# The last query chunk of a fused attention and FFN block, divided into two halves

## The chip, the cores and the metric

The kernel runs on one core of one Trainium2 chip. The metric is device time in microseconds (us) of one execution; a number of runs is taken and their median compared. Busy times, waits and clocks come from one profiled execution, a little apart from the runs.

## The reference

Input x has 2048 tokens of 512 numbers, in bf16. With layernorm without weights:

```python
x = A_x
h = x + _A_ref(_layernorm(x, axis=-1), A_wqkv, A_wo)      # 32 heads of 16, softmax over all 2048 keys
h2 = h + _B_ref(_layernorm(h, axis=-1), B_w_gate, B_w_up, B_w_down)

# _A_ref
scores = jnp.einsum("bhqd,bhkd->bhqk", q, k) * (Dh ** -0.5)
p = _softmax(scores, axis=-1)
o = jnp.einsum("bhqk,bhkd->bhqd", p, v)                   # then reshaped and multiplied by wo
# _B_ref, F = 1792
h = _sigmoid(g) * u                                       # g = x @ w_gate, u = x @ w_up
return jnp.einsum("bsf,fd->bsd", h, w_down)
```

## The kernel before

**Units and steps.** Queries are cut into four chunks of 512 (`QC`), the 32 heads into eight groups of four, the keys into 16 tiles of 128. A unit is one chunk, group, key tile and head: one score matmul (line 702) of 128 keys against 512 queries, which fills one PSUM bank. Units follow each other in the order chunk, group, key tile, head; three make a step, so there are 2048 units and 683 steps. A step's three banks lie in one of two score buffers `pss`, used in turn. ScalarE turns the three banks into bf16 probabilities with one exponential (line 711). In every fourth step, and in some more (the set `twice`), the third bank goes to VectorE instead, which works out the exponential in five operations spread over four steps (lines 730 to 743). The PV matmuls (line 769, four heads side by side in the array's columns, 17 columns each: 16 for values and one for the softmax sum) add into `acc`, mostly in one burst every fourth step.

**Queries in QB.** The score matmuls read their queries from one of two tiles `QB`, one for each head group in turn. It is filled by six DMAs on SyncE's queue: four for the rows (line 213) and two for a bound that is subtracted in the exponent (line 221). They are emitted while the group before is being scored, at its key tile 12 of 16.

**Normalising a group.** After the last PV matmul of a group, VectorE copies `acc` to `xs` (line 748). SyncE sends the four rows of sums to DRAM (`sd`), reads them back spread over the partitions (`s32`); five steps later VectorE takes reciprocals (line 757), and SyncE writes them to DRAM (`rd`) and spreads them by four DMAs (`rb`, line 762). Ten steps after the copy VectorE multiplies (line 763) into `OT`.

**Order of the work.** The program is written out by hand: a loop over steps emits a step's score matmuls, the PV matmuls due, what is due on VectorE and SyncE (`later`), then fillers. Each engine's queue, SyncE's among them, runs its instructions in that order. `emit_fill` takes fillers from one generator; `("at", n)` holds it until the next step with number n modulo 4, `("gap", n)` for n steps, `("from", n)` until step n.

**The FFN as filler.** Under the attention of a chunk, from its 16th step on, the output projection, layernorm, gate, up and down of the chunk before run as fillers (`ffn_tasks`). All their matmuls write to one PSUM bank, `pm`. wo: two halves of four matmuls and a transpose for each of four token tiles. Gate and up: 14 blocks of 128 rows of F; four gate matmuls in a step 3, a tanh on ScalarE (line 496), four up matmuls in the next step 1, a product on VectorE (line 500). Down: five matmuls in a cycle of four steps. Nothing is left to hide the last chunk's FFN: `ffn_last` runs it behind the loop, with six PSUM banks. Of the last chunk's first token tile seven of eight wo matmuls are done inside the loop (`wo_early`); `spin` issues matmuls whose results are not used.

Of the kernel before, what the change touches and what calls it, by code (L numbers as in the profile page):

```python
# [2 lines left out]

# [14 lines left out]
def kernel(  # L18
# [11 lines left out]
    nc = tc.nc  # L30
# [10 lines left out]
    TQ = QC // P  # L41
    NQC = S // QC
# [64 lines left out]
    stg = const.tile([P, 2 * S], BF16)  # L107
    stages = [stg[:, 0:S], stg[:, S:2 * S]]
# [97 lines left out]
    qgs = [(qc, g) for qc in range(NQC) for g in range(NG)]  # L206

    def emit_q_rows(n):
        qc, g = qgs[n]
        assert ("q", qc, g // 2) in ready  # L210
        for j in range(4):
            r = 64 * (g % 2) + DH * j
            nc.sync.dma_start(out=QB[n % 2][32 * j:32 * j + 32:2, j, :],
                              in_=QTu[r:r + DH, g // 2, qc * QC:(qc + 1) * QC])

    def emit_q_bound(n, engs=(nc.sync, nc.sync)):
        qc, g = qgs[n]
        assert ("b", qc, g // 2) in ready
        r = 32 * qc + 4 * g
        for h in range(2):  # L220
            engs[h].dma_start(out=QB[n % 2][64 * h + 1:64 * h + 2, 2 * h:2 * h + 2, :],
                              in_=bnd[r + 2 * h:r + 2 * h + 2, :])
# [151 lines left out]
    units = [(qc, g, kt, j) for qc in range(NQC) for g in range(NG) for kt in range(NT) for j in range(4)]  # L374
    groups = [units[i:i + GU] for i in range(0, len(units), GU)]
    NS = len(groups)
    SPC = NS / NQC

# [86 lines left out]
    def wo_mm(ps, t, g):  # L465
        nc.tensor.matmul(ps[:], lhsT=OT[t // TQ % 2][:, g, t % TQ * P:(t % TQ + 1) * P], rhs=wo_pad[:, g, :],  # L466
                         start=(g == 0), stop=(g == NG - 1))
# [18 lines left out]
    def gate_mm(ps, f, c):  # L486
        nc.tensor.matmul(ps[:], lhsT=wg[:, c, f * P:(f + 1) * P], rhs=hnT[:, c, :],  # L487
                         start=(c == 0), stop=(c == DC - 1))

    def up_mm(ps, f, c):  # L490
        nc.tensor.matmul(ps[:], lhsT=wu[:, c, f * P:(f + 1) * P], rhs=hnT[:, c, :],  # L491
                         start=(c == 0), stop=(c == DC - 1))
# [6 lines left out]
    def up_mul(ps, sg, f):  # L499
        nc.vector.scalar_tensor_tensor(out=hT[:, f, :], in0=sg[:], scalar=1.0, in1=ps[:],  # L500
                                       op0=ALU.add, op1=ALU.mult)
# [11 lines left out]
    def ffn_tasks(qc):  # L513
        yield ("rate", 8.0)
        for tt in range(TQ):
            xr = x_load(qc * TQ + tt)
            yield ("at", 3)
            ps = pm_tile()
            for g in range(NG):
                if g == NG // 2:  # L520
                    yield ("at", 1)
                yield 1
                wo_mm(ps, qc * TQ + tt, g)
# [5 lines left out]
        for f in range(FC):  # L529
            yield ("at", 3)  # L530
            psg = pm_tile()
            for c in range(DC):
                yield 1
                gate_mm(psg, f, c)
            sg = gate_act(psg)
            yield ("at", 1)
            psu = pm_tile()
            for c in range(DC):
                yield 1
                up_mm(psu, f, c)  # L540
            up_mul(psu, sg, f)
        for tt in range(TQ):
            for f in range(FC):
                if f % 5 in (0, 3):
# [5 lines left out]
            down_out(psd, qc * TQ + tt, tt)  # L550
        yield ("rate", None)
        yield ("gap", 1)
# [3 lines left out]
    def wo_early(qc):  # L556
        early[0] = pm_tile()
        for g in range(NG - 1):
# [3 lines left out]
            wo_mm(early[0], qc * TQ, g)  # L562
# [5 lines left out]
    def ffn_last(qc):  # L568
        t0 = qc * TQ
        sums, rb = pm_tile(), pm_tile()  # L570
        pss = [early[0]] + [pm_tile() for _ in range(TQ - 1)]
        tp = {}
        def wo(tt, g0, g1):
            for g in range(g0, g1):
                wo_mm(pss[tt], t0 + tt, g)
# [4 lines left out]
        wo(1, 0, NG - 1)  # L580
        xs = norm.tile([P, QC], FP32, name="xs")
        nc.vector.tensor_copy(out=xs[:], in_=acc[:])
        for q in range(TQ):
            nc.tensor.matmul(sums[:, 4 * q:4 * q + 4], lhsT=xs[:, q * P:(q + 1) * P],
                             rhs=ident_f[:, DH:P:32], start=True, stop=True)
        r16 = small.tile([P, 4 * TQ], FP32, name="r16")
        nc.vector.reciprocal(out=r16[:], in_=sums[:, 0:4 * TQ])
        rx = norm.tile([P, TQ, 4, 32], FP32, name="rb")
        wide = r16[:].rearrange("p (t j) -> p t j", j=4).unsqueeze(3).to_broadcast([P, TQ, 4, 32])
        nc.vector.tensor_copy(out=rx[:, 0:2], in_=wide[:, 0:2])  # L590
        nc.scalar.copy(out=rx[:, 2:4], in_=wide[:, 2:4])
        xrs = [x_load(t0 + q) for q in range(TQ)]
        wo(2, 0, NG - 1)
        for tt in range(TQ):
            nc.tensor.matmul(rb[:, tt * P:(tt + 1) * P], lhsT=rx[:, tt].rearrange("p j d -> p (j d)"),
                             rhs=ident_f[:], start=True, stop=True)
        nc.vector.tensor_tensor(out=OT[qc % 2][:, NG - 1, :], in0=xs[:], in1=rb[:], op=ALU.mult)
        add_x(0)
        add_x(1)
        wo(3, 0, 2)  # L600
        wo(0, NG - 1, NG)
        wo(1, NG - 1, NG)
        wo(3, 2, NG - 1)
        add_x(2)
        add_x(3)
        wo(2, NG - 1, NG)
        wo(3, NG - 1, NG)
        spin(acc, 5)
        mv = small.tile([P, TQ, nc.vector.BN_AGGR_DIM], FP32, name="mvl")
        nmr = small.tile([P, TQ], FP32, name="nmr")  # L610
# [13 lines left out]

        def turn(tt, copy):
            if tt % 2 == 0:
                tp[tt // 2] = pm_tile()[:].bitcast(BF16).rearrange("p (h b q) -> p h b q", h=2, b=4)
            pt = tp[tt // 2][:, tt % 2]
# [7 lines left out]
        stats(2)  # L636
# [3 lines left out]
        stats(3)  # L640
        apply(2)
        turn(1, nc.scalar.copy)
        spin(acc, 3)
        apply(3)
        turn(2, nc.vector.tensor_copy)
        spin(acc, 3)
        turn(3, nc.vector.tensor_copy)
        spin(acc, 2)
        for tt in range(TQ):
            nc.vector.tensor_copy(out=h_sb[:, tt, :], in_=pss[tt][:])  # L650
        for f in range(FC):
            psg = pm_tile()
            for c in range(DC):
                gate_mm(psg, f, c)
            sg = gate_act(psg)
            psu = pm_tile()
            for c in range(DC):
                up_mm(psu, f, c)
            up_mul(psu, sg, f)
        psd = [pm_tile() for _ in range(TQ)]  # L660
        for tt in range(TQ):
            for f in range(FC):
                down_mm(psd[tt], f, tt)
            down_out(psd[tt], t0 + tt, tt)

    def filler():
# [21 lines left out]
    def emit_scores(i):  # L688
# [8 lines left out]
        for ui, (qc, g, kt, j) in order:  # L697
            n_qg = qc * NG + g
# [3 lines left out]
            nc.tensor.matmul(pss[:, ui, :], lhsT=KT[rows, g, kt * P:(kt + 1) * P],  # L702
                             rhs=QB[n_qg % 2][rows, j, :], start=True, stop=True,
                             tile_position=(h0, 0) if pairs else None)
# [3 lines left out]
        k = i % 7  # L708
        pt = pt4[k] if k < 4 else (pt_early if i < GM else pt_late)[k - 4]
# [36 lines left out]
    def emit_norm(qc, g, i):  # L746
        xs = norm.tile([P, QC], FP32, name="xs")
        nc.vector.tensor_copy(out=xs[:], in_=acc[:])  # L748
        sd = dram.tile([4, QC], FP32, name="sd")
        for j in range(4):  # L750
            nc.sync.dma_start(out=sd[j:j + 1, :], in_=xs[32 * j + DH:32 * j + DH + 1, :])
        s32 = norm.tile([P, 16], FP32, name="s32")
        nc.sync.dma_start(out=s32[:], in_=sd[:].rearrange("j (a b) -> (j a) b", b=16))

        def recip():
            r32 = norm.tile([P, 16], FP32, name="r32")
            nc.vector.reciprocal(out=r32[:], in_=s32[:])
            rd = dram.tile([4, QC], FP32, name="rd")
            nc.sync.dma_start(out=rd[:].rearrange("j (a b) -> (j a) b", b=16), in_=r32[:])
            rb = norm.tile([P, QC], FP32, name="rb")  # L760
            for j in range(4):
                nc.sync.dma_start(out=rb[32 * j:32 * j + 32, :], in_=rd[j:j + 1, :].to_broadcast([32, QC]))
            later(i + 10, lambda: nc.vector.tensor_tensor(out=OT[qc % 2][:, g, :], in0=xs[:], in1=rb[:], op=ALU.mult))
        later(i + 5, recip)

    def emit_pv(qc, g, kt, i):
        assert ("v", kt) in ready
        for j in range(4):
            nc.tensor.matmul(acc[32 * j:32 * j + VW, :], lhsT=Vaug[:, kt, 4 * g + j, :],  # L769
                             rhs=p_of.pop((qc, g, kt, j)), start=(kt == 0), stop=(kt == NT - 1),  # L770
                             tile_position=(0, 32 * j))
        if kt == NT - 1 and (qc, g) != qgs[-1]:
            emit_norm(qc, g, i)


# [73 lines left out]
    with tc.manual_schedule():  # L849
# [32 lines left out]
        ffn_last(NQC - 1)  # L882
# [30 lines left out]
```

## Time and profile before

| What | Value |
|---|---|
| Median of 3 runs | 972.46 us (972.37 to 974.98) |
| Span of the profiled execution | 970.6 us; the profile lists no other time of its own |
| ScalarE busy | 894.9 us (92%) |
| TensorE busy | 836.9 us (86%), 5288 matmuls |
| VectorE busy | 798.0 us (82%) |
| GpSimd busy | 39.7 us (4%) |
| Mean granted TensorE clock | 0.998 |
| Score matmuls, line 702 | 2048 of 128x512, mean 381 ns |
| Exponentials on ScalarE, line 711 | 683 of 128x1536 or 128x1024 |
| tanh, line 496 | 56, mean 628 ns |
| QB rows, line 213 | 128 DMAs of 16 KB |

A matmul's duration holds its way through the array: matmuls that follow each other start closer together than they last. PE is TensorE's matmuls, PEld its weight loads, DVE VectorE, ACT ScalarE, POOL GpSimd, SP SyncE. Idle time of an engine that is not the bottleneck costs nothing. SPq marks the issue of a DMA on SyncE's queue; the transfer goes on after it.

### The profile page before, as it was taken

The numbers are of one execution on the slowest core, as the hardware profiler recorded it, in microseconds if no ns is written. First come the engines' busy times: TensorE is split into PE (matmuls) and PEld (weight loads), VectorE is DVE, ScalarE is ACT, GpSimd is POOL, SyncE is SP. The second block draws the span as 40 slices with busy tenths as digits, with TensorE's granted clock in tenths as the row PEclk, the third lists the DMA queues.
The fourth block names the chain that finished last, engine by engine and source line by source line (L and its number), as shares of the span: only waits on it lengthen the run. The fifth ranks groups of instructions, "written<-read, shape, count | busy, mean of one in ns | idle before, by whom it ended". The sixth has DMA issues, their size and how long they took to land.

```text
span 970.6 us, 14758 instructions
## 1 busy us (share of the span) xinstructions
PE 836.9 (86%) x5288; PEld 273.4 (28%) x5288; DVE 798.0 (82%) x1418; ACT 894.9 (92%) x773; POOL 39.7 (4%) x45
## 2 busy tenths in 40 slices
PE   4788888888888999988788999888788999998898
PEld 2221222222222232222222333222222223222343
DVE  9389999888878888889888888889878888889452
ACT  4799999999999999999999999999999999999731
POOL 4600000000000000000000000000000000000000
PEclk9999999999999999999999999999999999999999
DMA  5001341000003000000000000000000000000100
GB/s 160 20 1 56 113 94 37 15 16 5 16 23 101 15 15 16 20 19 28 4 26 27 16 16 15 21 8 26 16 26 26 16 16 14 8 25 24 34 2 22
DMA packets 32354, 28.07 MB, mean 29 GB/s; under 512 B 14300, under 2 KB 26716, under 8 KB 32280
## 3 DMA queue, kind: packets, MB, share of 16 engines
q1 hardware_dynamic: 30692, 25.56, 9.4%
q10 hardware_dynamic: 1588, 1.58, 0.5%
q8 instruction: 41, 0.67, 0.3%
q14 instruction: 33, 0.27, 0.1%
HBM read 20.18 MB, written 2.61 MB: 23 GB/s over the span
## 4 chain that ended last, share of the span: by engine, by line
PE 42%; DVE 28%; ACT 22%; issue 5%; DMA 2%; SPq 0%; ACTq 0%; POOL 0%; DVEq 0%
PE pss L702 20%; ACT pt L711 12%; PE acc L769 8%; ACT wd L711 4%; PE pm L491 4%; ACT stg L711 4%; DVE stg L730 4%; PE pm L487 3%; PE pm L504 2%; ACT QTu L711 2%; DVE pt L743 2%; DVE y L739 2%; DVE reg L733 2%; PE pm L466 2%; DVE st L130 2%
## 5 line engine op out<-in xcount | busy, mean ns | idle before, releaser
L702 PE MATMUL pss<-QB,KT 64*128 64x512 bf16 (+1 forms) x2048 | 470.8, 381 | 94.3 <-ACT pt L711 44.2
L711 ACT ACTIVATE pt<-pss 128x1536 bf16<-128x1536 f32 (+1 forms) x392 | 498.3, 1359 | 13.0 <-PE pss L702 10.7
L702 PEld LDWEIGHTS <-KT 64*128 64x128 bf16 (+1 forms) x2048 | 138.4, 95 | 377.6 <-issue 258.6
L711 ACT ACTIVATE stg<-pss 128x1536 bf16<-128x1536 f32 (+1 forms) x140 | 182.1, 1354 | 2.4 <-PE pss L702 0.9
L730 DVE TENSOR_SCALAR stg<-pss 128x512 int32<-128x512 f32 x123 | 84.7, 688 | 69.3 <-PE pss L702 58.5
L769 PE MATMUL acc<-pt,Vaug 128*17 128x512 bf16 x1175 | 113.0, 382 | 8.3 <-DVE xs L748 5.6
L711 ACT ACTIVATE wd<-pss 128x1536 bf16<-128x1536 f32 (+1 forms) x80 | 103.8, 1394 | 1.4 <-PE pss L702 1.3
L711 ACT ACTIVATE QTu<-pss 128x1024 bf16<-128x1024 f32 (+1 forms) x71 | 95.3, 1343 | 0.5 <-PE pss L702 0.2
L736 DVE SCALAR_TENSOR_TENSOR y<-reg 128x512 f32<-128x512 f32 x123 | 85.2, 693 | 4.2
L739 DVE SCALAR_TENSOR_TENSOR y<-y,reg 128x512 f32<-128x512 f32 x123 | 84.1, 684 | 1.1
L769 PEld LDWEIGHTS <-Vaug 128*17 128x17 bf16 x2048 | 39.3, 88 | 114.5 <-issue 96.6
L487 PE MATMUL pm<-reg,reg 128*128 128x512 bf16 x224 | 57.8, 380 | 6.0 <-DVE reg L500 6.0
L504 PE MATMUL pm<-wd,reg 128*128 128x512 bf16 x224 | 60.8, 381 | 0.5 <-DVE reg L500 0.5
L491 PE MATMUL pm<-reg,wu 128*128 128x512 bf16 x224 | 57.9, 381 | 0.0
L733 DVE TENSOR_SCALAR reg<-stg 128x512 int32<-128x512 int32 x123 | 52.1, 423 | 2.5
L137 POOL TENSOR_TENSOR rs<-ve,pw_neg 128x1 f32<-128x1 f32 (+1 forms) x24 | 17.1, 713 | 880.8 <-DVE ve L135 879.0
L496 ACT ACTIVATE sg<-pm 128x512 f32<-128x512 f32 x56 | 35.2, 628 | 18.0 <-PE pm L487 18.0
L769 PE MATMUL acc<-stg,Vaug 128*17 128x512 bf16 x420 | 50.5, 385 | 0.5 <-DVE xs L748 0.2
L500 DVE SCALAR_TENSOR_TENSOR reg<-sg,pm 128x512 bf16<-128x512 f32 x56 | 38.2, 682 | 14.0 <-PE pm L491 13.3
L743 DVE SCALAR_TENSOR_TENSOR pt<-y,stg 128x512 bf16<-128x512 f32 x70 | 47.8, 682 | 1.9
L730 DVE TENSOR_SCALAR wd<-pss 128x512 int32<-128x512 f32 x45 | 30.9, 686 | 13.1 <-PE pss L702 12.8
L156 PE MATMUL pm<-reg 128*128 128x512 bf16 x124 | 37.6, 391 | 1.2 <-DVE km L164 0.7
(115 smaller groups left out, 711.0 us busy)
## 6 DMA issues: line engine op xcount, KB each, us to landing
rb<-rd SPq DMA_DIRECT2D x124, 64.0 KB
reg<-in_A_x_dram SPq DMA_DIRECT2D x8, 256.0 KB
QB<-QTu SPq DMA_DIRECT2D x128, 16.0 KB
xr<-in_A_x_dram SPq DMA_DIRECT2D x16, 128.0 KB
out_dram<-ob SPq DMA_DIRECT2D x16, 128.0 KB
sd<-xs SPq DMA_DIRECT2D x124, 2.0 KB
KT<-stg SPq DMA_DIRECT2D x7, 256.0 KB
reg<-in_B_w_gate_dram SPq DMA_DIRECT2D x4, 448.0 KB
```

What stands on the lines that cost most here:

```text
L487: nc.tensor.matmul(ps[:], lhsT=wg[:, c, f * P:(f + 1) * P], rhs=hnT[:, c, :], start=(c == 0), stop=(c == DC - 1))
L491: nc.tensor.matmul(ps[:], lhsT=wu[:, c, f * P:(f + 1) * P], rhs=hnT[:, c, :], start=(c == 0), stop=(c == DC - 1))
L500: nc.vector.scalar_tensor_tensor(out=hT[:, f, :], in0=sg[:], scalar=1.0, in1=ps[:], op0=ALU.add, op1=ALU.mult)
L504: nc.tensor.matmul(ps[:], lhsT=hT[:, f, tt * P:(tt + 1) * P], rhs=wd[:, f, :], start=(f == 0), stop=(f == FC - 1))
L702: nc.tensor.matmul(pss[:, ui, :], lhsT=KT[rows, g, kt * P:(kt + 1) * P], rhs=QB[n_qg % 2][rows, j, :], start=True, stop=True, tile_positio ...
L711: ex = nc.scalar.activation(out=pt[:, 0:na, :], in_=pss[:, 0:na, :], func=ACT.Exp, scale=DH ** -0.5 / QS)
L730: return nc.vector.tensor_scalar(out=e_bits, in0=src, scalar1=ONE_BITS, scalar2=0.0, op0=ALU.add, op1=ALU.max)
L733: nc.vector.tensor_scalar(out=e_man, in0=e_bits, scalar1=0x7FFFFF, scalar2=-0x40800000, op0=ALU.bitwise_and, op1=ALU.bitwise_or)
L736: nc.vector.scalar_tensor_tensor(out=e_pol, in0=m, scalar=PA, in1=m, op0=ALU.add, op1=ALU.mult)
L739: nc.vector.scalar_tensor_tensor(out=e_pol, in0=e_pol, scalar=PB, in1=e_man.bitcast(FP32), op0=ALU.add, op1=ALU.mult)
L743: nc.vector.scalar_tensor_tensor(out=dst, in0=e_pol, scalar=PC, in1=e_bits.bitcast(FP32), op0=ALU.add, op1=ALU.mult)
L769: nc.tensor.matmul(acc[32 * j:32 * j + VW, :], lhsT=Vaug[:, kt, 4 * g + j, :], rhs=p_of.pop((qc, g, kt, j)), start=(kt == 0), stop=(kt == ...
```

## The change

The last chunk of 512 queries is divided into two of 256, so there are five chunks. In these two, a score bank holds two key tiles of 256 queries: a unit takes two score matmuls of 256 columns, an exponential sees as many columns as before, and the PV matmuls are twice as many with half the columns. A head group there has 8 x 4 units in place of 16 x 4, 10.7 steps in place of 21.3, and each group has its own QB rows, bounds and normalisation as before, so there are 16 groups in the last 171 steps instead of 8. QB rows are asked for at three quarters of a group's units (k 6 of 8). The tiles for normalisation are allocated once; in the half chunks the groups use their halves in turn.

The FFN of chunk 2 (512 queries) runs under the first half, from its 12th step on, that of the first half under the second. wo, layernorm and down use denser slots there (`ffn_wo_tight`, and three slots of three down matmuls in a cycle of four steps); for the first half gate and up take three slots in a cycle, each of eight 256-column matmuls, which fill a bank with two blocks of F. `ffn_last` now has 256 queries. The extra exponentials on VectorE (`twice`) end 14 steps into the second half: four fewer.

In the built program steps 0 to 511 stand as before. The fillers end at step 679, but for four of the seven early wo matmuls, which stand behind the loop. In the half chunks SyncE's queue holds, for each group, the four `sd`, the `s32`, then either `rd` and four `rb` and after them the six QB transfers, or the six first.

```diff
+    CHUNKS = [(0, QC), (QC, QC), (2 * QC, QC), (3 * QC, QC // 2), (3 * QC + QC // 2, QC // 2)]
+    NC = len(CHUNKS)
...
     def emit_q_rows(n):
-        qc, g = qgs[n]
-        assert ("q", qc, g // 2) in ready
+        c, g = qgs[n]
+        q0, w = CHUNKS[c]
+        assert ("q", q0 // QC, g // 2) in ready
         for j in range(4):
             r = 64 * (g % 2) + DH * j
-            nc.sync.dma_start(out=QB[n % 2][32 * j:32 * j + 32:2, j, :],
-                              in_=QTu[r:r + DH, g // 2, qc * QC:(qc + 1) * QC])
+            nc.sync.dma_start(out=QB[n % 2][32 * j:32 * j + 32:2, j, 0:w],
+                              in_=QTu[r:r + DH, g // 2, q0:q0 + w])
...
+    def n_k(c):
+        return NT // per_bank(c)
+
+    units = [(c, g, k, j) for c in range(NC) for g in range(NG) for k in range(n_k(c)) for j in range(4)]
...
+    def ffn_up(c):
+        w = CHUNKS[c][1]
+        at = cycle((3, 1) if c + 2 < NC else (3, 0, 1))
+        for fs in blocks_of(w):
+            yield ("at", next(at))
+            psg = pm_tile()
+            for i, f in enumerate(fs):
+                for k in range(DC):
+                    yield w / QC
+                    ffn_mm(wg, psg, w, f, i, k)
             sg = gate_act(psg)
...
+                if tight:
+                    if f % 3 == 0:
+                        yield ("at", (3, 0, 1)[at % 3])
+                        at += 1
+                elif f % 5 in (0, 3):
                     yield ("at", 0 if f % 5 else 3)
...
-        for qc in range(NQC - 1):
-            yield ("from", int((qc + 1) * SPC) + 15)
-            yield from ffn_tasks(qc)
-        yield from wo_early(NQC - 1)
+        for c in range(NC - 1):
+            yield ("from", int(first_step(c + 1)) + (11 if c + 3 >= NC else 15))
+            yield from ffn_tasks(c)
+        yield from wo_early(NC - 1)
...
-        for ui, (qc, g, kt, j) in order:
-            n_qg = qc * NG + g
+        n_of = max(per_bank(u[0]) for u in group)
+        parts = [(ui, u, h) for h in range(n_of) for ui, u in order[:2] if h < per_bank(u[0])]
+        parts += [(ui, u, h) for ui, u in order[2:] for h in range(per_bank(u[0]))]
+        for ui, (c, g, k, j), h in parts:
+            n_qg = c * NG + g
+            w = CHUNKS[c][1]
+            kt = k * per_bank(c) + h
...
-            nc.tensor.matmul(pss[:, ui, :], lhsT=KT[rows, g, kt * P:(kt + 1) * P],
-                             rhs=QB[n_qg % 2][rows, j, :], start=True, stop=True,
+            nc.tensor.matmul(pss[:, ui, h * w:(h + 1) * w], lhsT=KT[rows, g, kt * P:(kt + 1) * P],
+                             rhs=QB[n_qg % 2][rows, j, 0:w], start=True, stop=True,
                              tile_position=(h0, 0) if pairs else None)
-            if kt == 12 and j == 3 and n_qg + 1 < len(qgs):
+        for c, g, k, j in group:
+            n_qg = c * NG + g
+            if k == n_k(c) * 3 // 4 and j == 3 and n_qg + 1 < len(qgs):
                 emit_q_rows(n_qg + 1)
                 emit_q_bound(n_qg + 1)
...
+    def emit_pv(c, g, k, i):
+        w = CHUNKS[c][1]
+        for h in range(per_bank(c)):
+            kt = k * per_bank(c) + h
+            assert ("v", kt) in ready
+            for j in range(4):
+                p = p_of[(c, g, k, j)]
+                nc.tensor.matmul(acc[32 * j:32 * j + VW, 0:w], lhsT=Vaug[:, kt, 4 * g + j, :],
+                                 rhs=p[:, h * w:(h + 1) * w], start=(kt == 0), stop=(kt == NT - 1),
+                                 tile_position=(0, 32 * j))
...
-        for n in range(n0, min(int((qc + 1) * SPC) + 16, G1 - 8)):
+        for n in range(n0, min(int((qc + 1) * SPC) + 16, int(first_step(NC - 1)) + 14)):
             if n % ((4 if n < n0 + 56 else 3) * CYC) == 0:
                 twice.add(n + 2)
```

In `emit_norm` the DMAs and VectorE operations are the same in number, on 256 columns in the half chunks. In `ffn_last` the loops over token tiles run over two tiles instead of four, and of the seven wo matmuls of the second tile three stand ahead of the sums and four behind.

More of the change, by code (lines that the diff above doesn't have):

```diff
@@ L2 @@
 from contextlib import ExitStack
+from itertools import cycle
 import concourse.bass as bass
@@ L484, in hn_transpose, with blocks_of, ffn_mm @@
         transpose4(hnT[:, :, tt * P:(tt + 1) * P], hn, copy)
[L486 to L491, printed above, removed]
+    def blocks_of(w):
+        return [tuple(range(f, f + QC // w)) for f in range(0, FC, QC // w)]
+    def ffn_mm(wt, ps, w, f, i, c):
+        nc.tensor.matmul(ps[:, i * w:(i + 1) * w], lhsT=wt[:, c, f * P:(f + 1) * P], rhs=hnT[:, c, 0:w],
                          start=(c == 0), stop=(c == DC - 1))
@@ L577, in add_x @@
         def add_x(tt):
             nc.tensor.matmul(pss[tt][:], lhsT=ident_bf[:], rhs=xrs[tt][:], start=False, stop=False)
[L580 to L583, printed above, removed]
+        wo(1, 0, 3)
+        xs = norm_part(xs_all, w, NG - 1)
+        nc.vector.tensor_copy(out=xs, in_=acc[:, 0:w])
+        for q in range(n):
             nc.tensor.matmul(sums[:, 4 * q:4 * q + 4], lhsT=xs[:, q * P:(q + 1) * P],
@@ L585, in ffn_last @@
                              rhs=ident_f[:, DH:P:32], start=True, stop=True)
[L586 to L592, printed above, removed]
@@ L593, in ffn_last @@
-        wo(2, 0, NG - 1)
-        for tt in range(TQ):
+        wo(1, 3, NG - 1)
+        r16 = small.tile([P, 4 * n], FP32, name="r16")
+        nc.vector.reciprocal(out=r16[:], in_=sums[:, 0:4 * n])
+        rx = norm_part(rb_all, w, NG - 1).rearrange("p (t j d) -> p t j d", t=n, j=4)
+        wide = r16[:].rearrange("p (t j) -> p t j", j=4).unsqueeze(3).to_broadcast([P, n, 4, 32])
+        nc.vector.tensor_copy(out=rx[:, 0], in_=wide[:, 0])
+        nc.scalar.copy(out=rx[:, 1], in_=wide[:, 1])
@@ L606, in ffn_last @@
[L606 to L610, printed above, removed]
+        nc.vector.tensor_tensor(out=OT[c % 2][:, NG - 1, 0:w], in0=xs, in1=rb[:, 0:w], op=ALU.mult)
+        ready.add(("o", c, NG - 1))
+        for tt in range(n):
+            add_x(tt)
+        for tt in range(n):
+            wo(tt, NG - 1, NG)
+        spin(acc, 6)
+        mv = small.tile([P, n, nc.vector.BN_AGGR_DIM], FP32, name="mvl")
@@ L761, in recip @@
             for j in range(4):
-                nc.sync.dma_start(out=rb[32 * j:32 * j + 32, :], in_=rd[j:j + 1, :].to_broadcast([32, QC]))
-            later(i + 10, lambda: nc.vector.tensor_tensor(out=OT[qc % 2][:, g, :], in0=xs[:], in1=rb[:], op=ALU.mult))
+                nc.sync.dma_start(out=rb[32 * j:32 * j + 32, :], in_=rd[j:j + 1, :].to_broadcast([32, w]))
+            later(i + 10, scale)
         later(i + 5, recip)
[L766 to L773, printed above, removed]
+    def emit_pv(c, g, k, i):
+        w = CHUNKS[c][1]
+        for h in range(per_bank(c)):
[6 more added lines that the diff above has]
+                                 tile_position=(0, 32 * j))
+        if k == n_k(c) - 1 and (c, g) != qgs[-1]:
+            emit_norm(c, g, i)
```

192 lines of the change are left out of this document (112 added, 80 removed).

## The prediction

> **What bounds the kernel now.** Four views, in this order: the page, the table by stage, the chain that ended last, and the SyncE queue's timeline.
>
> ```profile
> PE   4788888888888999988788999888788999998898
> ACT  4799999999999999999999999999999999999731
> ```
>
> ScalarE is full from the second slice to the last three, so the attention loop ends when its exponentials end. The last slices belong to TensorE. The table by stage (columns: us, busy PE, PEld, DVE, ACT, POOL, then granted clock, DMA share, GB/s) cuts the end where the chain of waits changes engine:
>
> ```profile
> 756.85:832.95 76.10, 71.40 (x450) 22.77 (x448) 63.49 (x109) 75.38 (x70) 0.00 (x0) 1.00 0.05 15
> 832.95:892.05 59.10, 53.92 (x348) 16.55 (x345) 52.05 (x88) 58.47 (x49) 0.00 (x0) 1.00 0.07 20
> 916.84:930.75 13.91, 13.32 (x79) 7.00 (x79) 7.26 (x23) 4.27 (x7) 2.16 (x4) 1.00 0.13 40
> 930.75:955.09 24.34, 24.34 (x113) 11.06 (x113) 11.18 (x17) 8.36 (x14) 0.00 (x0) 1.00 0.00 1
> 955.09:970.60 15.51, 12.09 (x56) 5.29 (x54) 3.45 (x5) 0.00 (x0) 0.00 (x0) 0.97 0.10 34
> ```
>
> The chain of waits names the borders:
>
> ```profile
> 915.70 1.14 ACT pt L711
> 955.09 12.10 PE pm L504 x56
> ```
>
> The last exponential ends at 916.84, and 53.8 us of tail follow to 970.6, in which TensorE works alone on the last 512 queries. Ahead of that, the first two rows show ScalarE 99% busy and TensorE 94% with gate and up fillers, 91% with down fillers: the loop has little room on either engine.
>
> **The tail gets shorter.** Gate and up: 28 groups in 24.34 us, 0.87 each; 256 queries need 14 groups of eight 256-column matmuls, as many columns as a group now, so 12.2 us: minus 12.2. Down: 56 matmuls in 12.1, 0.216 each; 28 remain: minus 6.0. The first 13.9 us: the per-head sums, reciprocals and OT scaling run on half the columns, and two of four LayerNorm tiles, each with about 1.1 us of DVE steps in a row, go; but the seven wo matmuls that now stand ahead of the sums partly remain. I take 9.5, minus 4.4. The final 3.4 (last sum and its store) stays. Total minus 22.6 (ends minus 21.5 and minus 23.5).
>
> That needs 256-column matmuls at half the price. Here is the row nearest to it:
>
> ```profile
> 26.40 0.61 PE L288 MATMUL pm<-reg 128*128 128x256 bf16 x4
> ```
>
> One of them alone lasts 0.27, so four in 0.61 start 0.11 apart, with a full weight load each. The Trainium skill, "TensorE: Matmul & The Clock Gate", Part 3, says that a weight load overlaps running matmuls only when the row group differs; by that each would show its 0.097 us load and the 14 groups would take about 11 us more. The trace disagrees: loads of the same rows are hidden here.
>
> **The loop gets heavier.** Both kernels have 683 steps, steps 0 to 511 stand alike, and every step exponentiates as many columns. What is added under the loop: seven tanh, the FFN matmuls of 256 queries (about 22 us of TensorE), less four extra DVE exponentials in the last half chunk. I price four-step cycles by rows, from the starts of the exponentials. Without fillers a cycle takes 5.05 to 5.09; with down fillers 4.97; with gate and up (eight matmuls) 5.37 to 5.50, one tanh being 0.4 of that. A cycle with an extra DVE exponential takes 4.55 to 5.1, but the cycle behind it often 5.7 to 6.1, so I count their removal as nothing.
> - Steps 648 to 664: three slots in a cycle where the gate and up cycles have two. TensorE: 5.1 now, plus four matmul times of 0.216, is 5.9; psum tile pm is single, so each up group also waits for the tanh one step ahead: 6.2. Four cycles, 24.8 against 19.8 now: plus 5.0.
> - Denser down (steps 604 to 628, 668 to 680): 9 matmuls in a cycle, about 5.3: plus 1.3. Denser wo and LayerNorm, at 5.3: plus 1.0.
> Together plus 7 (ends plus 2, if ScalarE alone set the pace, and plus 13, if every hand-over of pm stalls). The fillers do end inside the loop, at step 679.
>
> **The query rows come late.** This is the largest term. A head group was 64 units, 21.3 steps; it is now 32, 10.7 steps, and has the same DMAs on SyncE: normalisation (four sd, s, rd, four rb), then four QB rows and two bounds. The rows of the next group are still asked for at three quarters of the group: four to five steps before their first use until now, one or two from now on. SyncE's queue goes in program order. One group of it in the timeline:
>
> ```profile
> 814.13 1.10 SPq L751 DMA_DIRECT2D sd<-xs  x4
> 816.22 0.34 SPq L753 DMA_DIRECT2D s<-sd  x1
> 819.75 0.34 SPq L759 DMA_DIRECT2D rd<-r  x1
> 821.17 1.71 SPq L762 DMA_DIRECT2D rb<-rd  x4
> 822.93 2.46 SPq L213 DMA_DIRECT2D QB<-QTu  x4
> 825.76 1.28 SPq L221 DMA_DIRECT2D QB<-bnd  x2
> ```
> ```profile
> 819.48 0.25 DVE L757 RECIPROCAL r<-s 128x16 f32<-128x16 f32 x1
> ```
>
> The first bound is issued 6.28 us after the reciprocal. What issue to use costs is seen where TensorE waits for one, at the start (SyncE issue, then the matmul):
>
> ```profile
> 32.25 0.70 SPq L221 DMA_DIRECT2D QB<-bnd  x1
> 34.13 0.37 PE L702 MATMUL pss<-QB,KT 64*128 64x512 bf16 x1 [0.72 <-DMA QB<-bnd]
> ```
>
> That is 1.88, so QB is usable 8.16 after the reciprocal. The reciprocal is emitted five steps after the norm, and this one started 0.6 ahead of its step's exponential. In the changed kernel's order, three cases take turns. In five of the groups (norm at steps 514, 546, 578, 610, 642) rd and rb stand ahead of the rows, and the new group begins three steps after the reciprocal, which is 4.04 us in this stretch. The exponential of that step is then late by 8.16 + 0.4 (its matmuls) - 0.6 - 4.04 = 3.9 us; other reciprocals lie up to 1.1 us on either side. TensorE stands at that score matmul, with the PV matmuls, all fillers and so VectorE's later work queued behind; ScalarE has nothing to read. Five times 4: plus 20. In five more (norm at 538, 570, 602, 634, 666) the rows stand ahead of rd, start when the s load is out, 3.1 us after the xs copy, and are usable about 8 us after the norm, six steps (7.6 to 8.1) being there: 0.5 each, plus 2.5. The others have a step more and wait for nothing. An out store (615) and an x load (636) that stand ahead of the rows add 0.5 each. Together plus 23.5. Nothing hides it; the ends are plus 14 (half-size transfers land sooner, and VectorE, rested, does its reciprocals a microsecond early) and plus 28. Below nothing is excluded, as the rows are never asked for earlier.
>
> **Clock.** Behind 36 us without fillers the granted clock fell, with no gap on TensorE over 1.1 us near it:
>
> ```profile
> 706.00:710.00 4.00, 2.69 (x21) 0.87 (x22) 3.64 (x7) 4.00 (x4) 0.00 (x0) 1.00 0.27 80
> 710.00:714.00 4.00, 3.73 (x19) 0.76 (x19) 2.62 (x5) 3.01 (x3) 0.00 (x0) 0.57 0.10 34
> ```
>
> The cycle around it took 6.19 where its neighbours take 5.08: 1.1 us for one drop. Five waits leave TensorE idle for over 4 us each; a wait may bring a drop or none, so 0 to 5.5, and I take two: plus 2. The Trainium skill, same page, "HAM oscillation", says that gaps beyond about 3.4 us halve the clock; by that all five would, plus 5.5. The drop here came without such a gap.
>
> **Sum.** -22.6 + 7 + 23.5 + 2 = +9.9. The span is 970.6, the profile gives no time around it, and the median of the runs, 972.46, lies 1.9 above it; I keep that. 970.6 + 9.9 + 1.9 = 982.4.
>
> **Rivals.**
> - *The rows come in time (faster).* If SyncE lets them out before rd, or TensorE is so far behind ScalarE that it asks later, the waits and drops go: 972.5 - 22.6 + 7 = 957. For it: no wait on QB shows after the start, and SyncE is idle for most of a group. Against: two score buffers keep TensorE at most two steps ahead, and SyncE's waits for the reciprocal stand in the rows above. It decides where the five waits and the 2.5 fall below 13 us together.
> - *Half the waits*, if groups with a wait push the next norm and reciprocal ahead of their step: 972.5 - 22.6 + 7 + 12 + 1 = 970, no change.
> - *TensorE pays more (slower still).* A quad of 256-column PV matmuls is not in the trace; a 512-column quad takes 0.216 (twelve matmuls, 0.65). If its four loads of 0.088 us set the pace, a half quad costs as much, 0.65 more in a cycle; in some 9 dense cycles, where TensorE sets the pace, plus 6; with five drops (plus 3.5 beyond my two), 992. For it: a half quad has half the time to hide its loads. Against: these loads start 3 ns apart, and L288 hides a 0.097 us load behind 256 columns.
>
> **How the numbers follow.** Forecast 0.70, rows in time 0.12, half the waits 0.10, TensorE 0.08. The forecast's own range, with its ends taken as independent (1, 5.5, 7 and 3 us, root of the squares 9.4), is 973 to 992. Down to 967 it takes in the half waits; rows in time are left out with the edges, some 0.2. A measurement of this kernel can tell about 0.3%, 2.9 us: slower is over 975.4, faster under 969.5. Of the forecast 0.64 is slower, 0.05 same, 0.01 faster; half the waits give 0.06 same and 0.04 faster. Slower 0.72, same 0.11, faster 0.17.
>
> **What would show it.** The chain of waits from the last exponential to the end 31 us, not 54: the tail. Score matmuls (the 256-column ones) with idle time "<-DMA QB<-bnd" or "QB<-QTu", five near 4 us and a few under 1, in all about 23: the rows; under 8 would make me wrong. ScalarE's idle time behind the score matmul of the same steps. Cycles in steps 648 to 664 near 6.2. The clock under 1 in some of the 4 us behind a wait. If the waits are there and the time is still lower, the loop's other terms were overpriced.

## The result, and the profile after

| | before | after |
|---|---|---|
| Median of the runs | 973.04 us (972.37 to 974.98, 4 runs) | 997.91 us (997.01 to 999.86, 4 runs) |
| Span of the profiled execution | 970.6 us | 995.7 us |
| Mean granted TensorE clock there | 0.998 | 0.982 |

The change makes the kernel slower: the ratio of the times is 1.026, with a 95% interval of 1.0241 to 1.0278. The direction and the places were foreseen, the size was not: plus 24.9 us where plus 9.9 was predicted, and above the range.

The rows of busy tenths of the page after, to be laid beside the two shown of before:

```profile
PE   4788888888888999987788999887788979798988
ACT  4799999999999999999999999999787979697872
PEclk9999999999999999999999999999898989899999
```

ScalarE, full to the last three slices before, now has five dents from slice 29 on. The clock row dips at the first four of them. The views of waits name what lies there. First, for what the score matmuls' engine sat idle, over the whole execution (us, times):

```profile
its engine sat idle before it (us, times) until:
  ACT pt L776: 39.5, 101
  DMA QB<-bnd: 21.9, 10
```

One of these ten is the wait at the start that both kernels have. The waits of all engines between 695 and 964 us (us in total, times, longest):

```profile
PE pss L765 <- DMA QB<-bnd: 21.1, 9, 4.4
...
ACT pt L776 <- PE pss L765: 18.9, 21, 4.7
...
ACT stg L776 <- PE pss L765: 13.8, 14, 4.5
```

TensorE waits 21.1 us for bounds of QB, and ScalarE waits for TensorE in the same steps. Of the nine waits five are long: 4.18, 4.25, 4.38, 4.37 and 2.23. One of them, as SyncE's queue and then TensorE's show it:

```profile
752.40 0.34 SPq L833 DMA_DIRECT2D rd<-r_all  x1
754.82 1.71 SPq L835 DMA_DIRECT2D rb_all<-rd  x4
756.58 2.46 SPq L221 DMA_DIRECT2D QB<-QTu  x4
759.08 1.26 SPq L231 DMA_DIRECT2D QB<-bnd  x2
```

```profile
755.89 0.60 PE L765 MATMUL pss<-QB,KT 128*128 128x256 bf16 x4
760.74 0.58 PE L765 MATMUL pss<-QB,KT 128*128 128x256 bf16 x2 [4.25 <-DMA QB<-bnd]
```

The reciprocal of that group started at 752.17, so QB is usable 8.57 us behind it, where the prediction had 8.16. The order is the one it named: `rd`, `rb`, rows, bounds, and TensorE at a standstill behind them.

The table by stage of the changed kernel (columns: us, busy PE, PEld, DVE, ACT, POOL, granted clock, DMA share, GB/s). The first five rows are the four-step cycles with the long waits, the sixth is three dense gate and up cycles, the next three are the tail:

```profile
704.88:715.20 10.32, 5.56 (x48) 2.77 (x48) 4.44 (x9) 5.22 (x6) 0.00 (x0) 0.67 0.16 43
754.70:766.64 11.94, 7.69 (x60) 3.60 (x56) 3.37 (x7) 5.97 (x7) 0.00 (x0) 0.71 0.07 14
805.13:817.50 12.37, 7.99 (x60) 3.67 (x57) 3.70 (x6) 5.87 (x5) 0.00 (x0) 0.72 0.07 15
856.18:869.18 13.00, 7.90 (x59) 3.67 (x59) 3.78 (x7) 5.37 (x5) 0.00 (x0) 0.74 0.09 24
906.78:917.51 10.73, 7.94 (x72) 5.14 (x72) 4.25 (x7) 5.87 (x6) 0.00 (x0) 0.84 0.06 17
917.51:937.72 20.21, 18.78 (x216) 13.59 (x216) 12.72 (x23) 18.15 (x17) 0.00 (x0) 1.00 0.04 10
963.62:973.65 10.03, 7.88 (x48) 3.83 (x48) 4.07 (x14) 2.29 (x4) 1.08 (x2) 1.00 0.10 28
973.65:986.04 12.39, 12.39 (x113) 11.06 (x113) 5.28 (x8) 4.18 (x7) 0.00 (x0) 1.00 0.01 1
986.04:995.70 9.66, 6.04 (x28) 2.52 (x26) 2.07 (x3) 0.00 (x0) 0.00 (x0) 0.96 0.08 27
708.14:714.97 6.83, 4.22 (x38) 1.99 (x38) 1.28 (x2) 2.61 (x2) 0.00 (x0) 0.50 0.10 26
```

The waited cycles take 10.3 to 13.0 us where a cycle without filler takes 5.05 and a dense one 6.7. In each the clock is under 1, and the last row shows how: 0.50 for 6.83 us at the first long wait. The same stands at 759.34, 810.54 and 861.74, and at 912.94, at the wait of 2.23, it is 3.41 us. The first four falls start inside their waits, the last 0.41 us behind its wait. The tail from the last exponential (963.62) to the end is 32.1 us, where it was 53.8.

**The account.** All of the change lies behind step 512, whose exponential starts at 694.34 before and at 695.12 after (plus 0.8; the program is the same up to there, but this execution has a fall of the clock at 35.71 that the one before lacks). From there to step 680 the loop takes 218.70 before and 264.78 after: plus 46.1. The rest of the loop gives back 0.1, the tail 21.7. 0.8 + 46.1 - 0.1 - 21.7 = 25.1, the difference of the spans. The experiments divide the 46.1.

### The profile page after: what moved, and what is told of

Same layout as the page of the kernel before. It is cut to its first block, busy times and chain, and to the rows that moved or that the text cites. A ratio compares the mean times of both kernels' runs of the same rounds, so it can differ in the third digit from the quotient of the medians.

```text
span 995.7 us, 17220 instructions
## 1 busy us (share of the span) xinstructions
PE 846.8 (85%) x6409; PEld 336.3 (34%) x6409; DVE 788.9 (79%) x1423; ACT 898.7 (90%) x770; POOL 39.0 (4%) x45
## 3 DMA queue, kind: packets, MB, share of 16 engines
HBM read 20.31 MB, written 2.61 MB: 23 GB/s over the span
## 4 chain that ended last, share of the span: by engine, by line
PE 43%; DVE 23%; ACT 23%; issue 6%; DMA 2%; SPq 2%; ACTq 0%; POOL 0%; DVEq 0%
PE pss L765 21%; ACT pt L776 13%; PE acc L846 8%; PE pm L514 6%; ACT wd L776 4%; ACT stg L776 4%; PE pm L530 3%; DVE stg L795 3%; ACT QTu L776 2%; PE pm L490 2%; DVE pt L808 2%; DVE y L804 1%; DVE reg L798 1%; DVE y L801 1%; DVE st L137 1%
## 5 line engine op out<-in xcount | busy, mean ns | idle before, releaser
L765 PE MATMUL pss<-QB,KT 64*128 64x512 bf16 (+3 forms) x2560 | 478.5, 340 | 104.8 <-ACT pt L776 39.5
L765 PEld LDWEIGHTS <-KT 64*128 64x128 bf16 (+1 forms) x2560 | 179.9, 96 | 369.5 <-issue 243.4
L846 PE MATMUL acc<-pt,Vaug 128*17 128x512 bf16 (+1 forms) x1471 | 114.7, 344 | 5.9 <-DVE xs_all L820 3.7
L846 PEld LDWEIGHTS <-Vaug 128*17 128x17 bf16 x2560 | 51.5, 90 | 99.3 <-issue 83.0
L514 PE MATMUL pm<-reg,reg 128*128 128x512 bf16 (+1 forms) x280 | 59.7, 345 | 6.5 <-DVE reg L527 6.3
L514 PE MATMUL pm<-reg,wu 128*128 128x512 bf16 (+1 forms) x280 | 58.6, 341 | 1.4 <-ACT sg L519 1.2
L846 PE MATMUL acc<-stg,Vaug 128*17 128x256 bf16 (+1 forms) x564 | 52.0, 334 | 0.8 <-DVE stg L808 0.4
```

The lines of the kernel that those rows point to most:

```text
L514: nc.tensor.matmul(ps[:, i * w:(i + 1) * w], lhsT=wt[:, c, f * P:(f + 1) * P], rhs=hnT[:, c, 0:w], start=(c == 0), stop=(c == DC - 1))
L765: nc.tensor.matmul(pss[:, ui, h * w:(h + 1) * w], lhsT=KT[rows, g, kt * P:(kt + 1) * P], rhs=QB[n_qg % 2][rows, j, 0:w], start=True, stop= ...
L846: nc.tensor.matmul(acc[32 * j:32 * j + VW, 0:w], lhsT=Vaug[:, kt, 4 * g + j, :], rhs=p[:, h * w:(h + 1) * w], start=(kt == 0), stop=(kt == ...
```

## The experiments

**The theory**: the waits on QB and the clock that falls behind them make the kernel slower; the denser fillers cost a little, and the tail gives what was predicted. **The rivals**: the loop is slower because its matmuls of 256 columns or its denser fillers cost more, and the waits only stand where time would be lost anyway; or the waits are the cost and the clock is not.

### The rows asked for early

```diff
-            if k == n_k(c) * 3 // 4 and j == 3 and n_qg + 1 < len(qgs):
+            ask = 0 if per_bank(c) > 1 else 12
+            if k == ask and j == 3 and n_qg + 1 < len(qgs):
```

> The changed kernel, but in the two half chunks the QB rows and bounds of the next group are asked for in the first steps of a group (k 0) and not at three quarters (k 6), so that on SyncE's queue they stand ahead of the norm, rd and rb of the group before. Theory (the rows are held on the queue behind rd, TensorE waits for them, and the idle time brings a clock drop): the 21.9 us of waits on QB and the five clock drops behind them go, and with them the 30 us that the five long cycles took beyond their neighbours: 963 to 970 against 997.9. Rival (the denser fillers and 256-column matmuls fill TensorE, and the waits only show where it would be late anyway): at most 5 us better, 993 to 998.

Measured: 967.32 us, 0.994 of before (0.9917 to 0.9963). TensorE's waits in the loop no longer have a line on QB; the longest that is left for the score matmuls is

```profile
PE pss L765 <- ACT pt L777: 5.0, 14, 0.6
```

and in the stretch shown above SyncE has let the bounds out by 757.17 (755.91 + 1.26), with the next group's sums and `rd` behind them:

```profile
753.40 2.46 SPq L221 DMA_DIRECT2D QB<-QTu  x4
755.91 1.26 SPq L231 DMA_DIRECT2D QB<-bnd  x2
758.61 1.09 SPq L824 DMA_DIRECT2D sd<-xs_all  x4
...
763.97 0.34 SPq L834 DMA_DIRECT2D rd<-r_all  x1
```

This edit is worth 30.6 us (997.91 - 967.32), more than the whole loss. The same change with its rows in time is 0.6% faster than before. What is left, the same matmuls and the same fillers, is the loop without waits: 235.66 us from step 512 to 680, so plus 17.0 against before. The only fall of the clock in its loop is one of 3.41 us at 710.25, as in the profile before.

### The same waits, with TensorE kept busy

Ahead of the first score matmul of the groups that wait, matmuls are issued whose result is overwritten.

```diff
+            if w < QC and (k, j, h, ui) == (0, 0, 0, 2):
+                spin(pss[:, ui, :], 18 if i < 640 else 9)
```

> The changed kernel with 18 matmuls (9 in the last place) of 512 columns, whose result is overwritten, ahead of the score matmul that waits in the five late groups: 3.9 us of work that fits into a wait of 4.2 us. The rows stay late. Theory (the clock falls to half because TensorE stands idle, and that costs about 11 us over the five): the clock stays at 1, the waits on QB become short in the profile but the exponentials come as late, and the time is 986 to 990. Rival (the clock drops cost nothing, since ScalarE sets the pace): 997 to 1000, as the dummy work can only delay.

Measured: 989.78 us, 1.0171 (1.0141 to 1.0202). TensorE's timeline at the group shown above, and the granted clock around it:

```profile
756.71 4.05 PE L633 MATMUL pss<-wo_pad,ident_bf 128*128 128x512 bf16 x18
760.60 0.38 PE L767 MATMUL pss<-QB,KT 128*128 128x256 bf16 x2
...
762.22 1.04 PE L514 MATMUL pm<-reg,reg 128*128 128x512 bf16 x3
```

```profile
752.00:764.00 12.00, 11.62 (x106) 6.24 (x102) 5.16 (x10) 8.48 (x9) 0.00 (x0) 1.00 0.07 14
```

The new group's rows still come late: its score matmul starts at 760.60, 8.03 us behind the reciprocal at 752.57, now at the end of the extra matmuls. But the clock stays at 1.00. The next gate group takes 1.04 us here (the trace has three of its four matmuls) and 1.89 at half the clock in the kernel after. The loop takes 256.65 us against 264.78, with no fall in it. So the falls behind the waits cost 8.1 us, by the loop and by the medians (997.91 - 989.78). The waits alone cost 256.65 - 235.66 = 21.0, close to the 21.1 of the waits' list; it would be about 1.4 more without the fall at 710.25, which the kernel with the early rows has in its loop and this one has not. The five long cycles shrink from 10.32, 11.94, 12.37, 13.01 and 10.73 to 9.03, 9.16, 10.86, 10.79 and 9.68. These five differences are not the price of one fall each, since single waits changed too: ScalarE's idle time ahead of the five late exponentials is 4.18, 4.19, 4.49, 4.67 and 2.39 after and 3.97, 3.52, 5.34, 4.47 and 2.96 here. Their sums, 19.9 and 20.3, are nearly the same, so the total holds.

### The rows on another queue

```diff
-            nc.sync.dma_start(out=QB[n % 2][32 * j:32 * j + 32:2, j, 0:w],
+            (nc.gpsimd if w < QC else nc.sync).dma_start(out=QB[n % 2][32 * j:32 * j + 32:2, j, 0:w],
...
-            engs[h].dma_start(out=QB[n % 2][64 * h + 1:64 * h + 2, 2 * h:2 * h + 2, 0:w],
+            (nc.gpsimd if w < QC else engs[h]).dma_start(out=QB[n % 2][64 * h + 1:64 * h + 2, 2 * h:2 * h + 2, 0:w],
```

> The changed kernel with the QB rows and bounds of the half chunks on GpSimd's queue, emitted at the same place as in the changed kernel (k 6). Theory (not the place in the program makes them late, but that they stand behind rd on SyncE's queue): GpSimd has nothing else queued there and lets them out as soon as the tile is free, the waits and the drops go, 963 to 972. Rival (asked for one or two steps ahead of use, they are late on any queue): the waits stay near 4 us, 993 to 1003.

Measured: 976.75 us, 1.0037 (1.0022 to 1.0053): 21 us better than after, and between the two expectations. The five long waits at SyncE's reciprocals are gone. Three others have come, 6.6 us in all, the longest 3.1. GpSimd's queue and then TensorE's show where:

```profile
739.62 0.59 POOL L144 TENSOR_TENSOR rs<-ve,pw_neg 128x1 f32<-128x1 f32 x1 [6.15 <-DVE ve L142]
740.17 2.01 POOL L221 DMA_DIRECT2D QB<-QTu  x4
742.17 1.00 POOL L231 DMA_DIRECT2D QB<-bnd  x2
```

```profile
743.81 2.29 PE L765 MATMUL pss<-QB,KT 128*128 128x256 bf16 x12 [3.07 <-DMA QB<-bnd]
```

GpSimd raises LayerNorm's variance to a power here, and waits 6.15 us for VectorE to deliver it; the rows stand behind. So what made the rows late is not the number of bytes nor the distance to their use alone, but what waits ahead of them on their queue, whichever queue that is. The Trainium skill, "Trainium Kernel Development and Optimization", Key Constraints, says that issuing DMAs from several engines only saves the sequencer's issue time. Here it saved 21 us, since an instruction that waits on a sequencer holds the DMAs behind it.

Of what this kernel takes beyond the one with the early rows, a part is not the edit's: the profiled execution has three falls of the clock ahead of step 512, where the program is the same, and starts that step 4.3 us later. Its loop is 5.7 us longer (241.36 against 235.66).

### The late rows in the kernel before

The reverse test: in the kernel before, the last chunk's rows are asked for at key tile 14, and the reciprocal and the scaling behind it are put off until three steps ahead of the new group.

```diff
-            if kt == 12 and j == 3 and n_qg + 1 < len(qgs):
+            if kt == (14 if qc == NQC - 1 else 12) and j == 3 and n_qg + 1 < len(qgs):
...
-            later(i + 10, lambda: nc.vector.tensor_tensor(out=OT[qc % 2][:, g, :], in0=xs[:], in1=rb[:], op=ALU.mult))
-        later(i + 5, recip)
+            later(i + 10 + lag - (lag > 0), lambda: nc.vector.tensor_tensor(out=OT[qc % 2][:, g, :], in0=xs[:], in1=rb[:], op=ALU.mult))
+        lag = (qgs.index((qc, g)) + 2) * 64 // GU - 3 - (i + 5) if qc == NQC - 1 and g < 6 else 0
+        later(i + 5 + lag, recip)
```

> The kernel before, undivided, with one thing of the changed one: in the last chunk the reciprocals and their DMAs are emitted three steps ahead of the group after next, and the QB rows behind them, for six groups (the scaling follows four steps later). Theory: six waits of about 4 us each on QB, and a clock drop behind most of them, 2 us each: plus 24 to 40, 997 to 1013. Rival (the waits need the half chunks, with their short groups and dense fillers): under 5 us more, 973 to 978.

Measured: 1009.47 us, 1.0388 (1.0353 to 1.0424). Nothing is halved in this kernel, and it shows the same line and the same fall of the clock:

```profile
PE pss L702 <- DMA QB<-bnd: 27.2, 7, 5.2
```

```profile
751.14:757.97 6.83, 5.35 (x22) 1.26 (x22) 0.21 (x1) 2.90 (x2) 0.00 (x0) 0.50 0.08 22
```

Its loop takes 255.84 us from step 512 to 680, 37.1 more than before; 27.2 are the waits, so the rest is 9.9. Each of its six long waits (3.64 to 5.17) brings a fall, three of them 6.83 us long and three 3.41, besides the one that before has too; no run here divides the 9.9 further. Waits of this kind cost this kernel the time although none of its score and PV matmuls is halved.

### What the dense gate and up cycles wait for

The loop's plus 17.0 is left. Two kernels, both with the rows early, take the dense gate and up cycles apart. In the first, each gate and up slot of the first half issues four of its eight matmuls (half of the contraction is left out).

```diff
-                for k in range(DC):
+                for k in (range(DC) if w == QC else (0, DC - 1)):
```

> The kernel with the early rows, and under the second half chunk the gate and up slots of the first half issue four matmuls instead of eight (half of the contraction is left out; tanh, products and order stay). It asks why the cycles with three gate and up slots take 6.7 us. Theory A (TensorE's matmuls fill the cycle): 1.3 us of matmuls less, and the cycles fall to ScalarE's pace, 5.4 to 5.7. Theory B (one PSUM bank pm, handed from matmuls to tanh or product and back, one step between slots): they stay at 6.3 or above.

In the second the slots are two in a cycle, as for the other chunks.

```diff
-        at = cycle((3, 1) if c + 2 < NC else (3, 0, 1))
+        at = cycle((3, 1))
```

> The kernel with the early rows, and gate and up of the first half in two slots of a cycle as everywhere else; eleven down matmuls and three wo matmuls more then fall behind the loop. If the third slot costs 1.3 us in a cycle beyond what it does, as the cycles of 6.7 against 5.37 say: 49.4 us from step 648 to 680 become about 43, and 3 come back behind the loop: 963 to 965 against 967.3. If three slots were as good as two with the spill: 967 to 970.

Three such cycles with the rows early, then with half the matmuls, then with two slots (the stages' table of each kernel, columns as above):

```profile
887.58:907.78 20.20, 18.78 (x216) 13.60 (x216) 12.90 (x24) 18.14 (x17) 0.00 (x0) 1.00 0.04 10
```

```profile
887.06:905.04 17.98, 14.96 (x180) 10.01 (x180) 13.25 (x24) 17.61 (x19) 0.00 (x0) 1.00 0.05 11
```

```profile
885.22:901.34 16.12, 15.54 (x194) 11.14 (x192) 11.96 (x22) 16.12 (x16) 0.00 (x0) 1.00 0.06 13
```

A cycle takes 6.73, 5.99 and 5.37 us. With two slots ScalarE is never idle (16.12 of 16.12) and a cycle costs what the same slots cost before the change, 5.37: the half-size score and PV matmuls add no time there. With three slots neither engine is full. Taking out 12 matmuls of a cycle gives back 0.74 of the 1.36; 0.62 stays. Half of that is ScalarE's own work. A tanh puts off the next exponential by 0.47 us, as these rows of the two-slot kernel show:

```profile
890.12 0.65 ACT L519 ACTIVATE sg<-pm 128x512 f32<-128x512 f32 x1
890.59 1.09 ACT L777 ACTIVATE stg<-pss 128x1024 bf16<-128x1024 f32 x1
```

The three cycles hold five tanhs with three slots and three with two, so ScalarE alone would take 5.37 + 2 x 0.48 / 3 = 5.69 us for a cycle with three slots. The half-gate kernel is 0.30 above that. Its 5.99 lies between the two accounts, nearer to A. I take the 0.30 to be the hand-over of `pm`; that is a reading of two kernels, and it was not tried with a second `pm`.

The first of these two kernels ran once, in 965.71 us. The second, which leaves nothing out, takes 965.14 us, 0.9928 (0.9916 to 0.994), the lowest median in this study. That is at the upper edge of the 963 to 965 expected. Its loop gives back 7.5 us (228.12 against 235.66): 6.4 in steps 648 to 680, as expected, and 1.4 in steps 524 to 548, where its profile lacks the fall at 710.25 (0.3 goes the other way between them). Behind the loop 11 down matmuls, 3 more of wo and an output store are left over, and the time from the last exponentials to the end grows by 5.3 us, where 3 was expected; a fall of the clock at 939.36 is in it:

```profile
926.60 2.50 PE pm L530 x11
```

### The fall of the clock that both kernels have

The profiles before and of the kernel with the early rows have one fall at 710.25, behind some 36 us without fillers. Matmuls of no use were put there, with the rows early, and then with two slots as well.

```diff
+            if 496 <= i < 523 and i % CYC in (1, 3):
+                spin(pm_tile(), 4)
```

> The kernel with the early rows, and four matmuls of 512 columns without use in every second step of the stretch without fillers (steps 496 to 522). Theory (the drop of the clock at 710 us, in this kernel and in the one before, comes from too little work on TensorE): no drop there, the cycle from step 524 falls from 6.6 to about 5.3, 965.5 to 966.5 against 967.3. Rival (the drop is not due to the load, or costs nothing): 967 to 968.

> Early rows, two slots for gate and up, and the useless matmuls of steps 496 to 522 together. If the two gains are separate they add: 961.5 to 964.

Measured: 972.02 us, 0.9992 (0.9974 to 1.001), and 968.72 us, 0.9962 (0.995 to 0.9975). Both miss: they are 4.7 and 3.6 us above the same kernels without the extra matmuls. The falls do not account for it: at a mean clock of 1.000 the first takes 968.9 to 969.7 us, the kernel with the early rows 965.5. The cycles that got them grew, from 5.39 to 5.68 and from 4.66 to 5.14 for instance, and the fall they were to prevent is absent in some executions anyway: the profiles of the half-gate and the two-slot kernels lack it without any extra matmul (the half-gate one has a fall at 881.72 instead). So these runs do not settle what sets that fall off; they show that eight spare matmuls in a cycle are not free where ScalarE sets the pace.

### No pause between the two FFNs

With two slots, the pause between the FFN of chunk 2 and that of the first half is left out, so that the fillers end four steps sooner.

```diff
-        yield ("gap", 1)
+        if c + 3 != NC:
+            yield ("gap", 1)
...
+            if c + 2 < NC:
+                yield ("from", int(first_step(c + 1)) + (11 if c + 3 >= NC else 15))
```

> Early rows, two slots for gate and up, and the first half's FFN begins right behind chunk 2's, four steps sooner (the pause between the two is left out). Two down matmuls instead of eleven fall behind the loop, nine of 0.216 us less there. If the spill is what the two-slot kernel pays behind the loop: 962 to 964 against 965.1. If the earlier wo and gate cycles cost as much as the spill: 965 to 966.

Measured: 965.76 us, 0.9937 (0.9916 to 0.9958). Against the two-slot kernel nothing can be told: the interval of the one lies within that of the other. Its profiled execution took 963.47, its others up to 968.47, and the mean clock of these goes from 0.999 down to 0.991. Two down matmuls are left behind the loop instead of eleven. In the profiles the tail is 3.3 us shorter and the loop 1.5 longer (229.62 against 228.12), but the medians do not show a gain.

## Why the prediction was right about the direction and wrong about the size

- **The tail** was right: minus 21.7 measured, minus 22.6 predicted. Gate and up take 12.39 us (12.2), down 6.06 (6.0), the first part 10.03 (9.5). The 112 matmuls of 256 columns start 0.111 us apart with a weight load each. By the rule on weight loads that the prediction set against the trace (the Trainium skill, "TensorE: Matmul & The Clock Gate", Part 3) this stage would have taken some 11 us more: here too the trace disagrees.
- **The query rows** were right: 21.1 us of waits against 23.5, five long ones and four small ones (1.7 together). Four of the long ones measured 4.18 to 4.38 where 4 was said; the fifth was 2.23. Asking early takes all of it away, and late rows bring it into the kernel before.
- **The clock was the first failed step.** "A wait may bring a drop or none, so 0 to 5.5, and I take two: plus 2." All five long waits brought a fall, and four of these are two pieces of 3.41 us long: nine pieces, which together cost 8.1, or 0.9 a piece. The price of one piece, 1.1, was near; the count was wrong, two where nine came, and the upper end, 5.5, allowed only five. The rule by which all five would come (the Trainium skill, same page, "HAM oscillation": gaps beyond about 3.4 us halve the clock) holds for the four gaps of 4.2 to 4.4; the drops behind 2.23 us and at 710.25 came without such a gap.
- **The denser fillers were the second, and the larger.** "Together plus 7 (ends plus 2 ... and plus 13)": 17.0 by the kernel with the rows early, above the upper end too. By its stages against before: gate and up (steps 648 to 664) 27.3 us against 19.8, plus 7.5 where 5.0 was said, as a dense cycle takes 6.7 and not 6.2. Denser wo and LayerNorm, for which one microsecond was said, cost 5.8: 35.6 against 31.8 in steps 524 to 548, 26.7 against 24.7 in 628 to 648. Denser down cost 33.1 against 31.1 in steps 604 to 628, and about 1.2 behind step 664, so 3.2 where 1.3 was said. Eight of its nine cycles (5.25 to 5.62) came near the 5.3 said, one took 6.30; and nine cycles at 5.3 against the 46.05 us that these steps take before are plus 1.65, so the 1.3 was too low by its own price. wo and LayerNorm were given the 5.3 of the down cycles. The 0.5 that is left lies in other steps. In steps 524 to 548 four token tiles now go through where two did: TensorE works 31.3 us there instead of 27.5, VectorE 30.1 instead of 24.3. No experiment isolates that stage; that the added work and its hand-overs through `pm` make its 3.8 us is argued.
- **The sum**: 0.8 + 17.0 + 21.1 + 8.0 - 0.1 - 21.7 = 25.1, where the prediction had 7 + 23.5 + 2 - 22.6 = 9.9. The two failed terms are 10 and 6 us too low. Of the two right ones the waits were put 2.4 too high and the gain of the tail 0.9 too high, and these two errors partly cancel.
- **The rivals.** *The rows come in time* falls as an account of this kernel; brought about by hand, it gives 967 and not 957, for the loop's price was too low in it as well. *Half the waits* falls: all of the waits are there. *TensorE pays more* was right in its five drops, wrong in its cause: half quads do not cost what whole ones do. Twelve PV matmuls of 512 columns in the kernel before, and 24 of 256 columns in the two-slot kernel, take the same time:

```profile
873.87 0.82 PE L769 MATMUL acc<-pt,Vaug 128*17 128x512 bf16 x12
```

```profile
881.92 0.83 PE L847 MATMUL acc<-pt,Vaug 128*17 128x256 bf16 x24
```

What stays open: what sets off a fall of the clock without a gap, what makes denser wo and LayerNorm cost 5.8 us, and whether the last 0.30 us of a dense gate and up cycle are the hand-over of the one PSUM bank.

## What to carry to other kernels

When a loop's groups are halved, a prefetch asked for at a fixed fraction of a group loses half its lead, while the chain of small DMAs ahead of it on the queue keeps its length: set the lead in time, and read on the queue's timeline what stands and waits ahead of it. An idle time of some microseconds on TensorE is not paid by its own length alone; add what the clock loses behind it, here one or two pieces of 3.41 us at about 0.9 us each. And price each kind of filler from its own stage: the third slot cost 1.36 us a cycle, and only 0.74 of it went away with the matmuls taken out.

## What the runs showed of the hardware

- The clock falls to 0.50 in pieces of 3.41 us, one or two of them, and the length of the gap does not decide which. In the kernel after, gaps of 4.18 to 4.38 us brought two and one of 2.23 brought one; in the kernel before with late rows, gaps of 4.93, 4.92 and 4.12 brought two, and gaps of 5.17, 4.11 and 3.64 one; with the rows on GpSimd's queue, gaps of 3.07 and 2.74 brought one.
- In each of these profiles all falls start whole numbers of 3.413 us apart: those of the kernel after at 708.14, 759.34, 810.54, 861.74 and 912.94, always 51.2 us, which is 15 pieces. How far a gap reaches past the start of the fall goes with the number of pieces in all thirteen cases: 0.82 to 2.61 us past it, two pieces; 0.37 or less, or ended before it, one.
- One such piece is 0.0018 of this kernel's mean clock (3.41 x 0.5 / 970), and the scatter of the runs goes with it. Runs of the kernel before took 971.1 to 971.5 us at a mean clock of 1.000, 971.6 to 972.8 at 0.998, 973.0 to 974.8 at 0.994 to 0.996, 974.7 to 976.0 at 0.991 to 0.993, and 978.8 at 0.987: about 1 us for a piece. Much of what looks like noise here is the number of these pieces.
- Four 256-column matmuls, each with a weight load of its own, start 0.11 us apart, and stay so in a block of 112.
